# Score and state products of a small attention chained in strict alternation

## The chip, the cores and the metric

The kernel runs as one program on one core of a Trainium2 chip. The metric is the device time of one execution in microseconds (us). TensorE does the matrix products, ScalarE (ACT) the activations, VectorE (DVE) and GpSimd (POOL) the elementwise work, and SyncE (SP) issues the transfers. TensorE loads a stationary operand (PEld in the profile) and then streams a moving operand through it (PE).

## The reference

The reference is an mLSTM recurrence over 2 batches, 8 heads, 768 positions and a head dimension of 40, followed by two dense feed-forward layers over 1536 tokens (320 to 2048 and back to 320).

```python
for t in range(S):
    m_new = np.maximum(f_gate[:, :, t] + m, i_gate[:, :, t])
    f_stab = np.exp(f_gate[:, :, t] + m - m_new); i_stab = np.exp(i_gate[:, :, t] - m_new)
    C = f_stab * C + i_stab * np.einsum('bhd,bhe->bhde', vt, kt)
    n = f_stab * n + i_stab * kt
    y[:, :, t] = sigmoid(o_gate) * (C @ qt) / np.maximum(np.abs(n @ qt), 1.0)
...
h = x @ w_in;  g = h - np.tanh(h);         x1 = g @ w_out      # layer 1
h = x1 @ w_in2; g = h * np.tanh(softplus(h)); out = g @ w_out2  # layer 2
```

## The kernel before

The recurrence is computed in 12 chunks of 128 positions: 6 positions times 2 batches, in the order (position 0, batch 0), (position 0, batch 1), (position 1, batch 0) and so on. They are called chunk 0 to chunk 11 here. A chunk is one run of `attention(j)`:

- Line 309 (293 to 303 for the first two chunks) makes the decay exponents `nb` in two PSUM banks, line 312 takes their exponential into `Dm` on ACT, and line 314 masks it on POOL.
- Lines 325 to 329 make the scores `sc` = K^T Q: eight products of 64 rows by 128 columns, one for each head, into two PSUM banks. Heads 0 to 3 lie on partitions 0 to 63 and write the first bank, heads 4 to 7 lie on partitions 64 to 127 and write the second. They are called the lower and the upper half here. The data are fp32, and each product runs as two passes: 12 chunks x 8 products x 2 passes = 192 instructions.
- Line 333 multiplies each bank into `Dm` on VectorE. Line 340 makes `it` from the carried state, line 351 `pv` = `Dm` V, and lines 354 to 367 normalise, gate and store the chunk in `xo`.
- Lines 370 to 372 make the state update `st`: eight products with 40 columns of weights. Even products write PSUM partitions 0 to 39, odd ones 64 to 103. Lines 379 and 380 fold them into the state `C`.

The scores, `nb`, `it`, `pv`, `st` and the transposes `xt` (line 254) share three PSUM banks (`ps_at`) after the first two chunks. A bank is given again when the engine that reads it is done.

The dense layers run beside this. Layer 1 takes blocks of two chunks (256 tokens): `mm1` (line 506) makes `h`, `tile1` the activation on ACT, VectorE and POOL, `mm2` (lines 565 to 567) sums into `acc`. Layer 2 takes three super blocks of 512 tokens. A weight passes through VectorE and ACT once before use (`conv_w`, lines 180 to 190, `raw` into `w`).

The order of the instructions on each engine is not written out. A scheduler places them by priority and by its own estimate of times, so a new ordering edge moves much else. `tc.issue_after` (in `after`, above line 140) is such an edge: the instruction goes behind another on the same engine, without a semaphore. `w_ps` products are fill, and their results are not used.

Of the kernel before, what the change touches and what calls it, by code (L numbers as in the profile page):

```python
# [1 line left out]

# [23 lines left out]
def kernel(  # L26
# [11 lines left out]
    nc = tc.nc  # L38
    B, P, _, HG, S = qk.shape
# [7 lines left out]
    HP = P // 2  # L47
# [87 lines left out]
    def after(x):  # L135
        e = ExitStack()
        for i in x:
            e.enter_context(tc.issue_after(i.ins))
        return e

    def copy_r(eng, o, x):
        if eng == 0:
            nc.scalar.activation(out=o, in_=x, func=AF.Copy)  # L143
        elif eng == 1:
            nc.vector.tensor_copy(o, x)
        else:
            nc.gpsimd.tensor_scalar(o, in0=x, scalar1=1.0, scalar2=0.0, op0=ALU.mult, op1=ALU.add)
# [6 lines left out]
    def load_w(n=1):  # L154
        for _ in range(n):
            if pending_loads:
                layer, f = pending_loads.pop(0)
                early = layer == 0 and f < ER
                t = (xp if early else rawp).tile(
                    [P, 2 * WC], U32, tag="x" if early else "raw", name="raw", bufs=NB - 1 if early else None  # L160
                )
                with after(spq):
                    x = nc.sync.dma_start(out=t, in_=(w1, w2)[layer][f].bitcast(U32))
                if layer == 0 and f < ER + 3:
                    spq[:] = [x]
                raw[layer, f] = t
# [3 lines left out]
    def conv_w(layer, f, first=(), behind=()):  # L170
        r = raw.pop((layer, f)).rearrange("p (n t) -> p n t", t=2)
        lo32, z = r[:, :, 0], r[:, :, 1]
        zf = z.bitcast(F32)
        w = wp.tile([P, WT], F32R, tag="w", name="w")
        wf = w.bitcast(F32)

        with after(first):
            nc.vector.tensor_scalar(lo32, in0=lo32, scalar1=29, scalar2=None, op0=ALU.logical_shift_right)  # L180
        nc.vector.scalar_tensor_tensor(lo32, in0=z, scalar=0x80000000, in1=lo32, op0=ALU.bitwise_and, op1=ALU.bitwise_or)  # L181
        scaled[layer, f] = nc.scalar.activation(out=zf, in_=zf, func=AF.Copy, scale=2.0 ** -111)  # L182
        with after(behind):
            third[layer, f] = nc.vector.scalar_tensor_tensor(  # L184
                z, in0=z, scalar=3, in1=lo32, op0=ALU.logical_shift_left, op1=ALU.bitwise_or
            )
        cvd[:] = [nc.scalar.activation(out=w[:, 0:WC], in_=zf, func=AF.Copy)]  # L187
        eng = nc.gpsimd if layer == 0 and f < PRE else nc.vector
        eng.tensor_tensor(w[:, WC:WT], in0=zf[:, 0:REM0], in1=wf[:, 0:REM0], op=ALU.subtract)  # L189
        eng.tensor_tensor(w[64:P, REM0:REM1], in0=zf[64:P, REM0:REM1], in1=wf[64:P, REM0:REM1], op=ALU.subtract)  # L190
        wtile[layer, f] = w
# [43 lines left out]
    def at_ps(shape, name):  # L235
        p, tag = at_pools[0]
        if len(at_pools) > 1:
            at_pools.append(at_pools.pop(0))
        return p.tile(shape, F32, tag=tag, name=name)
# [29 lines left out]
    def attention(j):  # L269
# [3 lines left out]
        hp = lambda t, h, d=D: t[HP * (h // HG):HP * (h // HG) + d, h % HG, :]  # L273
# [14 lines left out]
        for hf in range(2):  # L288
            nb = at_ps([P, HG, L], "nb")
            flat = nb.rearrange("p g s -> p (g s)")  # L290
            if c < EC:
                bh = b * H + HG * hf
                nc.tensor.matmul(
                    flat, lhsT=na[c], rhs=sel[:, bh:bh + HG].rearrange("p (g o) -> p g o", o=1).to_broadcast([P, HG, L]),
                    start=True, stop=False,
                )
                for hh in range(HG):
                    nc.tensor.matmul(
                        nb[:, hh, :], lhsT=sel[:, bh + hh:bh + hh + 1].to_broadcast([P, P]), rhs=n0[c], start=False,
                        stop=False,  # L300
                    )

                x = nc.tensor.matmul(
                    nb, lhsT=identr, rhs=cm.rearrange("p (o s) -> p o s", o=1).to_broadcast([P, HG, L]), start=False,
                    stop=True,
                )
# [13 lines left out]
        if c + 1 < NCH:  # L320
            wv = ap_.tile([P, H, D1], F32, tag="wv", name="wv", bufs=2)
# [1 line left out]
            copy_r(2, dl, Dm[:, :, L - 1:L])  # L323
            dls[:] = [nc.gpsimd.tensor_tensor(wv, in0=v, in1=dl.to_broadcast([P, H, D1]), op=ALU.mult)]
        scs = [at_ps([P, HG, L], "sc") for _ in range(2)]
        for hh in range(HG):
            for r, sc in enumerate(scs):
                h = HG * r + hh
                x = nc.tensor.matmul(sc[:, hh, :], lhsT=hp(kT, h, HP), rhs=hp(q, h, HP), start=True, stop=True)  # L329
        yield  # L330
        for r, sc in enumerate(scs):
            d4 = Dm[:, HG * r:HG * r + HG, :]
# [4 lines left out]
        if c > 0:  # L337
            it = at_ps([P, HG, 2, D1], "it")
            for g in range(HG):
                nc.tensor.matmul(  # L340
                    it[:, g].rearrange("p h d -> p (h d)"), lhsT=q[:, g, :],
                    rhs=C[:, g].rearrange("p h d -> p (h d)"), start=True, stop=True,
# [7 lines left out]
        for h in range(H):  # L350
            x = nc.tensor.matmul(pv[:, h, :], lhsT=Dm[:, h, :], rhs=v[:, h, :], start=True, stop=True)  # L351
# [3 lines left out]
        else:  # L355
# [6 lines left out]
        x = xo[:, j, 0:DM].rearrange("p (h d) -> p h d", h=H)  # L362
        nc.vector.tensor_tensor(x, in0=hv[:, :, 0:D], in1=x, op=ALU.mult)
        gated[j] = nc.vector.scalar_tensor_tensor(
            x, in0=x, scalar=1 / WS, in1=den.to_broadcast([P, H, D]), op0=ALU.mult, op1=ALU.mult
# [2 lines left out]
        yield  # L368
        if c + 1 < NCH:
            st = at_ps([P, HG, D1], "st")  # L370
            for h in [HG * r + g for g in range(HG) for r in range(2)]:
                nc.tensor.matmul(hp(st, h), lhsT=k[:, h, :], rhs=wv[:, h, :], start=True, stop=True)
            for r in range(2):
                sl = slice(HP * r, HP * r + D)
                if c == 0:
                    copy_r(0, C[sl, :, r, :], st[sl])
                else:
                    dc = dec[sl, b, :, c:c + 1].to_broadcast([D, HG, D1])
                    nc.gpsimd.tensor_tensor(C[sl, :, r, :], in0=C[sl, :, r, :], in1=dc, op=ALU.mult)
                    nc.vector.tensor_tensor(C[sl, :, r, :], in0=C[sl, :, r, :], in1=st[sl], op=ALU.add)  # L380
# [217 lines left out]
    def program():  # L598
# [56 lines left out]
        new_xT(0, 0)  # L655

        ga, gb = (attention(j) for j in blk[0, 0])

        def go(g, n=1):
# [44 lines left out]
        def attend():  # L704
            for k in range(1, NB):
                js = blk[0, k]
                gens = [(n, attention(j)) for n, j in enumerate(js)]
                if k < NB - 1:
                    new_xT(0, k)
                loads_to(js[0] + 1)  # L710
                while gens:
                    for n, g in list(gens[:2]):
                        loads_to(js[n] + 2)
                        if next(g, 0) == 0:
                            gens.remove((n, g))
                            if k < NB - 1:
                                yield
                                transpose_x(0, k, n)
                        yield
            left.close()  # L720
            late["x"] = pool(left, "lateX", 1, reuse_waits="tile")
            late["A"] = pool(left, "lateA", 2, reuse_waits="tile")
            yield from trans(0, NB - 1)
# [163 lines left out]
```

## Time and profile before

| | us |
|---|---|
| median of 3 runs | 468.28 (468.02 to 468.96) |
| profiled execution | 467.47 |
| its span, first to last instruction | 465.6 |
| TensorE busy | 450.6 |
| VectorE busy | 320.8 |
| ACT busy | 285.6 |
| POOL busy | 115.1 |

The profile's page is one execution, and its span leaves out 1.87 us around the first and last instruction. The ends of matrix products are modelled, so TensorE counts as busy while it drains. Recurrence and layer 1 share the time up to about 284 us, layer 2 takes the rest.

### The profile page before, as it was taken

How to read it: one execution, taken by the hardware profiler on the slowest of the kernel's cores; microseconds unless marked ns; L12 is line 12 of the kernel's file. 1: busy time of each engine (PE TensorE's matmuls, PEld its weight loads, DVE VectorE, ACT ScalarE, POOL GpSimd, SP SyncE). 2: the span in 40 equal slices, each digit the busy share in tenths (PEclk: the TensorE clock that was granted, in tenths of full speed). 3: DMA queues.
4: the chain of work that ended last, by engine and by line, in shares of the span. 5: the costliest groups of instructions: out<-in, count | busy, mean ns of one | idle time of the engine just before them, and what ended most of it. 6: DMA issues, size and time to landing. Idle time of an engine off the chain costs nothing.

```text
span 465.6 us, 8007 instructions
## 1 busy us (share of the span) xinstructions
PE 450.6 (97%) x3103; PEld 408.6 (88%) x3103; DVE 320.8 (69%) x546; ACT 285.6 (61%) x518; POOL 115.1 (25%) x121
## 2 busy tenths in 40 slices
PE   9969979999999999999999999999999999999996
PEld 5646869999989999999999989998889999988995
DVE  7997999989888887666889977989932221221121
ACT  6878556596665865888889687676643333332331
POOL 3314535575354431342433332000000000000000
PEclk9997999999999999999999999999999999999999
DMA  7965454513506111000110110445301000010001
GB/s 251 356 241 163 136 164 131 179 34 109 164 4 182 34 59 63 1 1 1 63 64 0 63 63 1 132 140 175 114 1 56 2 0 1 2 56 0 1 0 56
DMA packets 22744, 38.03 MB, mean 82 GB/s; under 512 B 1364, under 2 KB 17044, under 8 KB 22708
## 3 DMA queue, kind: packets, MB, share of 16 engines
q1 hardware_dynamic: 22708, 37.54, 24.6%
q8 instruction: 24, 0.39, 0.3%
q14 instruction: 12, 0.10, 0.1%
HBM read 35.41 MB, written 1.97 MB: 80 GB/s over the span
## 4 chain that ended last, share of the span: by engine, by line
PE 61%; DVE 21%; issue 8%; ACT 4%; POOL 3%; DMA 1%; POOLq 0%; ACTq 0%; SPq 0%; DVEq 0%
PE h L506 26%; PE acc L565 8%; PE acc L566 8%; PE acc L567 8%; DVE raw L184 3%; PE sc L329 3%; DVE raw L181 2%; POOL gl L519 2%; PE pv L351 2%; DVE w L189 2%; DVE raw L180 2%; DVE w L190 2%; DVE gl L548 2%; DVE g L535 1%; DMA raw<-in_w_dram 1%
## 5 line engine op out<-in xcount | busy, mean ns | idle before, releaser
L506 PE MATMUL h<-xT,w 128*128 128x256 f32 (+1 forms) x1152 | 211.1, 324 | 5.8 <-ACT w L187 2.7
L506 PEld LDWEIGHTS h<-xT,w 128*128 128x128 f32 x1152 | 169.7, 190 | 23.4 <-ACT w L187 4.2
L565 PE MATMUL acc<-w,gh 128*128 128x320 f32 x384 | 118.6, 312 | 0.8 <-DVE xo L582 0.8
L566 PE MATMUL acc<-w,gh 128*128 128x320 f32 x384 | 118.1, 310 | 0.0
L567 PE MATMUL acc<-w,gl 128*128 128x320 f32 x384 | 108.9, 310 | 0.0
L519 POOL TENSOR_TENSOR gl<-g,gh 128x512 fp32r<-128x512 f32 x48 | 66.0, 1378 | 120.7 <-ACT gh L143 116.3
L548 DVE TENSOR_TENSOR gl<-g,gh 128x512 fp32r<-128x512 f32 x48 | 33.1, 690 | 87.1 <-ACT g L547 87.0
L546 ACT ACTIVATE gh<-h 128x512 fp32r<-128x512 f32 x48 | 28.7, 598 | 77.1 <-PE h L506 74.2
L565 PEld LDWEIGHTS acc<-w,gh 128*128 128x128 f32 x384 | 72.1, 188 | 3.5 <-ACT w L187 0.9
L566 PEld LDWEIGHTS acc<-w,gh 128*128 128x128 f32 x384 | 72.2, 188 | 2.3
L567 PEld LDWEIGHTS acc<-w,gl 128*128 128x128 f32 x384 | 69.4, 188 | 1.6 <-issue 0.4
L535 DVE COPY_PREDICATED g<-u,t 128x512 f32<-128x512 uint32 x48 | 40.4, 844 | 10.1 <-ACT u L534 9.9
L532 DVE TENSOR_TENSOR g<-u,h 128x512 f32<-128x512 f32 x48 | 32.7, 680 | 16.9 <-ACT u L531 13.4
L143 ACT ACTIVATE gh<-g 128x512 fp32r<-128x512 f32 x48 | 30.5, 635 | 19.5 <-DVE g L535 15.2
L534 ACT ACTIVATE u<-u,bias 128x512 f32<-128x512 f32 x48 | 34.9, 728 | 11.4 <-DVE g L532 11.4
L187 ACT ACTIVATE w<-raw 128x704 fp32r<-128x704 f32 x32 | 27.7, 864 | 15.5 <-DVE raw L184 15.3
L529 ACT ACTIVATE u<-h 128x512 f32<-128x512 f32 x48 | 28.5, 593 | 11.6 <-PE h L506 11.6
L182 ACT ACTIVATE raw<-raw 128x704 f32<-128x704 f32 x32 | 27.6, 864 | 11.1 <-DVE raw L181 10.0
L533 DVE TENSOR_TENSOR t<-h,t 128x512 f32<-128x512 f32 x48 | 32.7, 682 | 0.0
L184 DVE SCALAR_TENSOR_TENSOR raw<-raw 128x704 uint32<-128x704 uint32 x32 | 30.9, 966 | 2.5 <-ACT raw L182 2.3
L531 ACT ACTIVATE u<-u 128x512 f32<-128x512 f32 x48 | 30.6, 637 | 0.0
L189 DVE TENSOR_TENSOR w<-raw,w 128x576 fp32r<-128x576 f32 x30 | 27.4, 913 | 3.0 <-ACT w L187 2.5
(103 smaller groups left out, 497.7 us busy)
## 6 DMA issues: line engine op xcount, KB each, us to landing
raw<-in_w_dram SPq DMA_DIRECT2D x32, 704.0 KB
qk_t<-in_qk_dram SPq DMA_DIRECT2D x12, 512.0 KB
kv_t<-in_kv_dram SPq DMA_DIRECT2D x12, 324.0 KB
out_dram<-xo SPq DMA_DIRECT2D x12, 160.0 KB
xo<-in_og_dram SPq DMA_DIRECT2D x2, 640.0 KB
xo<-in_og_dram SPq DMA_DIRECT2D x2, 320.0 KB
sd<-nr SPq DMA_DIRECT2D x20, 4.0 KB
md<-nr SPq DMA_DIRECT2D x10, 8.0 KB
```

Of the source, the lines that this page charges most:

```text
L184: third[layer, f] = nc.vector.scalar_tensor_tensor(z, in0=z, scalar=3, in1=lo32, op0=ALU.logical_shift_left, op1=ALU.bitwise_or)
L189: eng.tensor_tensor(w[:, WC:WT], in0=zf[:, 0:REM0], in1=wf[:, 0:REM0], op=ALU.subtract)
L506: y = nc.tensor.matmul(t[:, k * nt:(k + 1) * nt], lhsT=w[:, o:o + P], rhs=x[:, kk, :], start=(n == 0), stop=(n == len(pairs) - 1),)
L519: nc.gpsimd.tensor_tensor(gl, in0=g, in1=gh.bitcast(F32), op=ALU.subtract)
L532: mark[:] = [nc.vector.tensor_tensor(g, in0=u, in1=h, op=ALU.mult)]
L533: nc.vector.tensor_tensor(t, in0=h, in1=t, op=ALU.subtract)
L534: nc.scalar.activation(out=u, in_=u, func=AF.Relu, bias=bias[:, 0:1])
L535: nc.vector.copy_predicated(out=g, mask=u.bitcast(U32), data=t)
L548: mark.append(nc.vector.tensor_tensor(gl, in0=g, in1=gh.bitcast(F32), op=ALU.subtract))
L565: nc.tensor.matmul(a, lhsT=gh[:, sl], rhs=wh, start=(f in ends_), stop=False)
L566: nc.tensor.matmul(a, lhsT=gh[:, sl], rhs=wl, start=False, stop=False)
L567: nc.tensor.matmul(a, lhsT=gl[:, sl], rhs=wh, start=False, stop=(f + 1 in ends_ or f == NF - 1))
```

## The change

The score and the state products are issued through a helper that puts each one behind the one before it on TensorE. For the scores the pairs are also turned round: the upper half goes first. The state products had the two column positions in turn in the code already. No arithmetic, tile or transfer changes.

```diff
+    @contextmanager
+    def alternate():
+        done = []
+
+        def turn(issue):
+            with after(done[-1:]):
+                done.append(issue())
+
+        yield turn
...
-        for hh in range(HG):
-            for r, sc in enumerate(scs):
-                h = HG * r + hh
-                x = nc.tensor.matmul(sc[:, hh, :], lhsT=hp(kT, h, HP), rhs=hp(q, h, HP), start=True, stop=True)
+        with alternate() as turn:
+            for hh in range(HG):
+                for r in (1, 0):
+                    h = HG * r + hh
+                    turn(lambda: nc.tensor.matmul(scs[r][:, hh, :], lhsT=hp(kT, h, HP), rhs=hp(q, h, HP), start=True, stop=True))
...
-            for h in [HG * r + g for g in range(HG) for r in range(2)]:
-                nc.tensor.matmul(hp(st, h), lhsT=k[:, h, :], rhs=wv[:, h, :], start=True, stop=True)
+            with alternate() as turn:
+                for h in [HG * r + g for g in range(HG) for r in range(2)]:
+                    turn(lambda: nc.tensor.matmul(hp(st, h), lhsT=k[:, h, :], rhs=wv[:, h, :], start=True, stop=True))
```

What the scheduler makes of it is read from the order of the instructions. The first place is TensorE at chunk 10 (161 to 165 us in the trace of before). `sc_1978` is the bank of the lower half, `sc_1979` that of the upper. Before:

```order
L309 MATMUL nb_1974<-md_96,sd1_95 128x512
L329 MATMUL sc_1978<-qk_t_1531 128x128 x4
L506 MATMUL h_1988<-xT_1515,w_351 128x256
L506 MATMUL h_1988<-xT_1515,w_359 128x256 x8
L506 MATMUL h_2055<-xT_1515,w_382 128x256 x2
L329 MATMUL sc_1979<-qk_t_1531 128x128 x4
```

and in the changed kernel:

```order
L319 MATMUL nb_1974<-md_96,sd1_95 128x512
L340 MATMUL sc_1979<-qk_t_1531 128x128
L518 MATMUL h_1988<-xT_1515,w_351 128x256
L518 MATMUL h_1988<-xT_1515,w_359 128x256 x8
L518 MATMUL h_2055<-xT_1515,w_382 128x256 x8
L340 MATMUL sc_1978<-qk_t_1531 128x128
L340 MATMUL sc_1979<-qk_t_1531 128x128
L340 MATMUL sc_1978<-qk_t_1531 128x128
L340 MATMUL sc_1979<-qk_t_1531 128x128
L340 MATMUL sc_1978<-qk_t_1531 128x128
L340 MATMUL sc_1979<-qk_t_1531 128x128
L340 MATMUL sc_1978<-qk_t_1531 128x128
```

Before, four products of one half stood together, then, behind eleven of `h`, four of the other. Now one product of the upper half stands alone, and the other seven come together, in turn. Chunks 7, 8, 9 and 11 read the same in both kernels, with other work between; so do chunks 3 and 5. Chunks 0 and 1 alternated already, and chunk 4, which had its two fours one right behind the other, alternates now in one piece of eight.

The second place is TensorE at chunk 6 (102 to 104 us). `sc_1213` is the lower half, `sc_1214` the upper. Before:

```order
L567 MATMUL acc_1042<-w_631,gl_1108 128x320
L329 MATMUL sc_1213<-qk_t_737 128x128 x3
L329 MATMUL sc_1214<-qk_t_737 128x128 x3
L329 MATMUL sc_1213<-qk_t_737 128x128
L329 MATMUL sc_1214<-qk_t_737 128x128
L565 MATMUL acc_1041<-w_641,gh_1107 128x320
```

and in the changed kernel:

```order
L340 MATMUL sc_1214<-qk_t_737 128x128
L518 MATMUL h_1284<-xT_721,w_392 128x256
L518 MATMUL h_1402<-xT_721,w_446 128x256
L340 MATMUL sc_1213<-qk_t_737 128x128
L340 MATMUL sc_1214<-qk_t_737 128x128
L340 MATMUL sc_1213<-qk_t_737 128x128
L340 MATMUL sc_1214<-qk_t_737 128x128
L340 MATMUL sc_1213<-qk_t_737 128x128
L340 MATMUL sc_1214<-qk_t_737 128x128
L340 MATMUL sc_1213<-qk_t_737 128x128
```

Here all eight products stood in one piece, partly in turn, and now one is split off in front. Chunk 2 goes the same way.

The third place is VectorE at chunk 10, where `Dm` is multiplied by the two banks and `g` and `t` belong to the activation of layer 1. Before:

```order
L532 TENSOR_TENSOR g_1946<-u_1944,h_1927 128x512
L533 TENSOR_TENSOR t_1945<-h_1927,t_1945 128x512
L333 TENSOR_TENSOR Dm_1917<-sc_1978,Dm_1917 128x512
L535 COPY_PREDICATED g_1946<-u_1944,t_1945 128x512
L333 TENSOR_TENSOR Dm_1917<-sc_1979,Dm_1917 128x512
L532 TENSOR_TENSOR g_2007<-u_2005,h_1988 128x512
L533 TENSOR_TENSOR t_2006<-h_1988,t_2006 128x512
```

and in the changed kernel:

```order
L544 TENSOR_TENSOR g_1946<-u_1944,h_1927 128x512
L545 TENSOR_TENSOR t_1945<-h_1927,t_1945 128x512
L547 COPY_PREDICATED g_1946<-u_1944,t_1945 128x512
L344 TENSOR_TENSOR Dm_1917<-sc_1979,Dm_1917 128x512
L544 TENSOR_TENSOR g_2007<-u_2005,h_1988 128x512
L545 TENSOR_TENSOR t_2006<-h_1988,t_2006 128x512
L344 TENSOR_TENSOR Dm_1917<-sc_1978,Dm_1917 128x512
```

The upper bank is read first now, and both readings stand later in VectorE's order. The state products of chunks 0 and 1 moved ahead of `pv` of their own chunk on TensorE, and elsewhere they stand as they did. On the other engines the orders move by a few positions as well, above all between chunk 2 and chunk 7.

## Rows read from the trace of the kernel before

**Rows 1.** Windows: stretch in us, its length, busy PE, PEld, DVE, ACT, POOL; clock.

```profile
40.00:60.00 20.00, 18.79 (x156) 16.30 (x156) 19.74 (x30) 11.58 (x20) 12.32 (x15) 1.00 0.46 140
60.00:80.00 20.00, 17.44 (x135) 15.14 (x135) 19.56 (x38) 13.79 (x29) 8.98 (x10) 1.00 0.47 150
80.00:100.00 20.00, 19.77 (x175) 18.70 (x175) 19.10 (x38) 13.64 (x27) 9.89 (x9) 1.00 0.44 140
120.00:180.00 60.00, 60.00 (x494) 56.73 (x493) 50.39 (x93) 38.61 (x76) 25.31 (x26) 1.00 0.26 82
220.00:260.00 40.00, 40.00 (x313) 39.99 (x312) 36.81 (x60) 33.98 (x62) 14.39 (x11) 1.00 0.16 54
```

**Rows 2.** Chain that ended last: start us, length us, work.

```profile
49.55 1.27 DVE Dm L333 x2
...
117.63 0.44 PE st L372 x16
...
161.32 1.09 PE sc L329 x8
...
182.22 1.41 PE h L506 x12
...
328.12 0.60 DVE gl L548
```

**Rows 3.** Who TensorE waited for from 180 us on: total us, times, longest.

```profile
PE acc L565 <- DVE xo L582: 0.8, 1, 0.8
PE h L506 <- ACT w L187: 0.6, 2, 0.3
```

**Rows 4.** TensorE's timeline, chunk 10: start us, length us, work, passes.

```profile
161.25 1.16 PE L329 MATMUL sc<-qk_t 64*128 64x128 f32 x8
162.34 1.55 PE L506 MATMUL h<-xT,w 128*128 128x256 f32 x11
163.82 1.16 PE L329 MATMUL sc<-qk_t 64*128 64x128 f32 x8
```

**Rows 5.** TensorE's timeline, chunk 0.

```profile
8.49 1.16 PE L329 MATMUL sc<-qk_t 64*128 64x128 f32 x16
9.58 0.33 PE L298 MATMUL nb<-n,sel 128*128 128x128 f32 x1
```

**Rows 6.** Chunk 10 cut at 161.6 and at 162.1, and its last pass alone.

```profile
161.25 0.60 PE L329 MATMUL sc<-qk_t 64*128 64x128 f32 x3
...
161.25 1.04 PE L329 MATMUL sc<-qk_t 64*128 64x128 f32 x7
...
162.14 0.27 PE L329 MATMUL sc<-qk_t 64*128 64x128 f32 x1
```

**Rows 7.** TensorE's timeline, chunk 6.

```profile
102.67 1.49 PE L329 MATMUL sc<-qk_t 64*128 64x128 f32 x16
104.08 0.41 PE L565 MATMUL acc<-w,gh 128*128 128x320 f32 x1
```

**Rows 8.** TensorE's timeline, chunks 2 and 3; in brackets idle time and releaser.

```profile
45.94 1.17 PE L329 MATMUL sc<-qk_t 64*128 64x128 f32 x16
...
50.28 1.16 PE L329 MATMUL sc<-qk_t 64*128 64x128 f32 x8 [0.83 <-DVE Dm L333]
```

**Rows 9.** TensorE's timeline, chunk 4.

```profile
68.54 2.42 PE L329 MATMUL sc<-qk_t 64*128 64x128 f32 x16 [0.46 <-ACT Dm L312]
```

**Rows 10.** The start: timelines of POOL, TensorE and VectorE.

```profile
12.32 1.28 POOL L324 TENSOR_TENSOR wv<-kv_t,dl 128x328 f32<-128x328 f32 x1
...
16.35 1.09 PE L351 MATMUL pv<-kv_t,Dm 128*128 128x41 f32 x8
...
18.45 0.15 DVE L359 TENSOR_SCALAR den<-pv 128x8 f32<-128x8 f32 x1
```

**Rows 11.** VectorE's timeline, chunk 10.

```profile
165.08 0.69 DVE L333 TENSOR_TENSOR Dm<-sc,Dm 128x512 f32<-128x512 f32 x1 [0.62 <-PE sc L329]
165.69 0.68 DVE L532 TENSOR_TENSOR g<-u,h 128x512 f32<-128x512 f32 x1
```

More of the change, by code (lines that the diff above doesn't have):

```diff
@@ L1 @@
-from contextlib import ExitStack
+from contextlib import ExitStack, contextmanager
 import concourse.bass as bass
```

## The prediction

> **What bounds the kernel now.** I read the windows first. From 40 to 100 us VectorE is the full engine: it is busy for 19.74, 19.56 and 19.10 of each 20 us, while TensorE has idle time. From about 100 us on it is the other way round: in 120 to 180 us TensorE is busy for all 60.00 us and VectorE for 50.39 [rows 1]. The chain that ended last says the same. Up to 97 us its pieces are mostly VectorE's, such as `Dm` at 49.55. Behind that nearly all are TensorE's, the scores of chunk 10 among them with 1.09 us for eight passes [rows 2]. From about 285 to 335 us the chain lies on VectorE once more, as at 328.12 [rows 2], where layer 2 starts and its weights are converted. Yet TensorE hardly stands still for it: its waits from 180 us to the end sum up to 1.4 us [rows 3]. So what is taken off TensorE behind 97 us should show in the time nearly in full, and what is taken off before should show little. Chunks 6 to 11 lie behind that point, chunks 2 to 5 before it.
>
> **What a score product costs.** The cut timeline gives the pace inside a group of one half [rows 6]. Three passes end at 161.25 + 0.60 = 161.85, seven at 161.25 + 1.04 = 162.29, so four more passes take 0.44 us: 0.11 us a pass. The third pass starts at 161.85 less a pass's own length of 0.27, that is at 161.58; the first two slots took 0.33 us, so the first alone took 0.22. The last pass starts at 162.14, and `h` follows at 162.34 [rows 4], so it holds TensorE for 0.20. A visit to the scores with n slots therefore costs 0.11n + 0.20 us: 1.08 for eight, and the rows have 162.34 - 161.25 = 1.09 [rows 4].
>
> The neighbours pay too. Eleven passes of `h` between the two visits take 163.82 - 162.34 = 1.48 us [rows 4]; at the pace of 1.41 us for twelve [rows 2] they would take 1.29. So leaving and entering again cost 0.19 us, and a visit costs about 0.39 us beyond its slots.
>
> Where the halves alternate, two passes share a slot: chunk 0 takes 9.58 - 8.49 = 1.09 us for sixteen passes [rows 5], what eight passes of one half take.
>
> On the 0.39 us: the Trainium skill, "TensorEngine Tiling (Array Packing)", Key Properties, states that a change of the tiling mode, not of the tile alone, drains TensorE. By that rule a product that is split off pays for a visit of its own, which speaks against this change. The rows agree. If no drain were paid, chunk 6 below would come out at -0.22 in place of +0.29, and the sum at -3.6 in place of -3.1.
>
> **The change, chunk by chunk.** Chunks 7 to 11 (five) had two visits of four products, 2 x 1.09 = 2.18 us. Now they have a visit of one product (two slots, 0.42) and one of seven. There the four lower products need eight slots, and the three upper ones can lie beside them: 1.09. Together 1.51, a saving of 0.67 each, 3.35 us in all; the number of visits, and so the neighbours' cost, is the same. No row shows a group of seven. At best it takes seven slots, 0.97; at worst nothing overlaps behind the lone product, 14 x 0.11 + 0.20 = 1.74. I take 1.09, since chunk 0 is the nearest row.
>
> Chunk 6 had all eight in one visit, partly in turn: 104.08 - 102.67 = 1.41 us [rows 7]. Now it is 1.51 and one visit more for the neighbours, 0.19: a loss of 0.29. Behind 97 us the sum is -3.35 + 0.29 = -3.06 us.
>
> Before 97 us: chunk 2 was already one visit of 1.17 us length like chunk 0 [rows 8, 5], and loses 1.51 + 0.19 - 1.09 = 0.61. Chunks 3 and 5 save 0.67 each. Chunk 4 had its two fours behind one another with a wait inside, 2.42 us long [rows 9] against 1.16 for a visit in turn, and saves up to 1.26. That is 2.0 us less TensorE work, but VectorE sets this stretch, so I count it at nothing. At best the change takes away all of VectorE's idle time from 40 to 100 us, 0.26 + 0.44 + 0.90 = 1.6 us [rows 1]. The other way, VectorE's new order there costs what the third rival says.
>
> The state products gain nothing: sixteen passes take 0.44 us [rows 2], 0.03 a pass, so they were in turn and overlapping already. In chunks 0 and 1 they are moved ahead of `pv`. Some 22 passes at 0.03 us put 0.6 us in front of the second `pv`. That one ends at 16.35 + 1.09 = 17.44 and VectorE reads it at 18.45 [rows 10]; this 1.0 us hides them. Without that cover the start is 0.6 us longer. `wv`, for which they wait, is ready at 13.60 [rows 10], before TensorE would come to the last of them.
>
> The two readings of `Dm` by VectorE move behind the activation that stood beside them. At chunk 10 VectorE waited for the second half of the scores anyway, 0.62 us, and took up `g` of the next tile at 165.69 [rows 11]. With the lone product and 17 passes of `h` in front, the seven start at about 161.25 + 0.42 + 17 x 0.1175 + 0.19 = 163.86 and end at 164.95, when VectorE can go on as it did. I count nothing here.
>
> **The sum.** The profiled execution took 467.47 us. Less 3.06 this is 464.4. A tenth, 0.3 us, I take as lost again in 220 to 335 us, where VectorE has only 3.2 of 40 us free [rows 1] and TensorE meets its waits [rows 3] earlier: 464.7. The median of the runs, 468.28, lies 0.8 us above the profiled execution, so the forecast for the median is 465.5, or 0.6% faster. Its own range is 463.9 to 467.1: half of the saving lost at one end, the gain before 97 us at the other.
>
> **Rivals.**
>
> 1. The stretch before 97 us gains as well. For it: TensorE idled there on VectorE and ACT, as at chunks 3 and 4 [rows 8, 9], and has 2.0 us less to do. Against: VectorE is at 97%. With 1.6 us more the time is 463.9, and with layer 2 following in full 463.6. Chance 0.16.
>
> 2. The saving is made and given back: TensorE is earlier behind 97 us, but VectorE and ACT, whose orders moved too, hand over `g`, `xo` and the converted weights no earlier. For it: VectorE at 92% in 220 to 260 us [rows 1], and the chain on it around 328 us [rows 2]. Against: only 1.4 us of waits from 180 us on [rows 3]. The 1.4 us would grow to 4.5, and the time stays at about 468.2. Chance 0.18.
>
> 3. Slower: the second bank. In the second chunk of each pair (3, 5, 7, 9, 11) one product can start once ACT has read its exponents, but the other seven stand behind the bank that VectorE frees by its `Dm` of the chunk before. Four of them ran ahead of that wait until now. TensorE issues in order, so `h` and `acc` stand behind it, and ACT and VectorE behind those. Price: chunk 3 waited 0.83 us there already [rows 8]; if the 1.09 us of the four is uncovered each time, that is 5.4 us, less 3.1 saved, and the time is 470.6. It decides from 0.6 us a pair (3.06 / 5). For it: VectorE takes `Dm` late in its new order. Against: behind 97 us TensorE did not wait once at this place. Chance 0.14.
>
> 4. It doesn't do what it says: behind the lone product the seven don't overlap. Chunks 7 to 11 stay at 0.42 + 1.74 = 2.16, chunk 6 loses 0.42 + 1.74 + 0.19 - 1.41 = 0.94, and the time is 469.1. Against it: chunk 0 [rows 5]. Chance 0.03.
>
> **How the numbers follow.** The forecast has the remaining 0.49. The range of 462.9 to 469.0 leaves out the far end of the first rival and most of the third, under 0.2 together. About 0.2%, 0.94 us, is what a measurement of this kernel can tell from no change. Faster, below 467.3, are the forecast nearly whole, the first rival and a little of the second: 0.65. Within 0.2% is the second for the most part: 0.18. Slower are the third, the fourth and the end of the second: 0.17.
>
> **What would show it.** In chunks 7 to 11 a score row of two passes should be followed 0.42 us later by other work, and one of fourteen passes 1.09 us later. If the fourteen take 1.7, the fourth rival holds. Measured from the beginning of chunk 6, layer 2 should start about 3 us earlier than before. Idle time in front of the seven, put down to `Dm`, speaks for the third rival; larger waits on `xo` or `w` behind 220 us for the second. The forecast is wrong if chunk 6, which began at 102.67 us [rows 7], begins more than 2 us later.

## The result, and the profile after

The changed kernel takes 471.47 us (median, 470.77 to 473.11), the kernel before 468.15 us beside it: ratio 1.0076, 95% interval 1.0056 to 1.0096. It is slower by 3.3 us, where 2.8 us less was forecast. The profiled execution took 470.77 us with a span of 468.2, against 467.47 and 465.6. In this section and below, medians and ratios leave out five executions that lie over 1.5% above the quickest of their kernel at a lower granted clock; each is named where it belongs.

At the scores TensorE does what was predicted. The timeline at chunk 10 (start us, length us, work, passes) has the lone product, 17 passes of `h`, and the group of seven:

```profile
163.32 0.48 PE L340 MATMUL sc<-qk_t 64*128 64x128 f32 x2
163.74 2.25 PE L518 MATMUL h<-xT,w 128*128 128x256 f32 x17
165.91 1.16 PE L340 MATMUL sc<-qk_t 64*128 64x128 f32 x14
167.00 0.42 PE L577 MATMUL acc<-w,gh 128*128 128x320 f32 x1
```

Two passes are followed 0.42 us later, fourteen 1.09 us later, where four products of one half took 1.09 before [rows 4]. Chunk 6, the one that was to lose, reads:

```profile
107.77 0.48 PE L340 MATMUL sc<-qk_t 64*128 64x128 f32 x2
108.19 0.50 PE L518 MATMUL h<-xT,w 128*128 128x256 f32 x2
108.62 1.16 PE L340 MATMUL sc<-qk_t 64*128 64x128 f32 x14
109.70 0.41 PE L577 MATMUL acc<-w,gh 128*128 128x320 f32 x1
```

But it begins at 107.77 us, not 102.67 [rows 7]. The loss lies ahead of it. The windows (stretch, its length, busy PE, PEld, DVE, ACT, POOL, then the granted clock) answer to [rows 1]:

```profile
40.00:60.00 20.00, 19.14 (x142) 16.09 (x142) 19.61 (x32) 13.12 (x23) 12.25 (x15) 1.00 0.48 152
60.00:80.00 20.00, 15.09 (x116) 12.45 (x115) 14.44 (x29) 11.10 (x23) 5.47 (x9) 0.83 0.48 157
80.00:100.00 20.00, 20.00 (x189) 19.18 (x187) 19.71 (x37) 12.83 (x24) 6.63 (x7) 1.00 0.38 111
120.00:180.00 60.00, 60.00 (x525) 56.36 (x524) 52.31 (x99) 38.81 (x76) 25.17 (x28) 1.00 0.30 89
220.00:260.00 40.00, 40.00 (x313) 39.97 (x313) 35.36 (x61) 33.75 (x62) 14.06 (x10) 1.00 0.14 46
```

In 60 to 80 us TensorE is busy for 15.09 us (17.44 before), VectorE for 14.44 (19.56 before), and the granted clock is 0.83 (1.00 before). TensorE's timeline says where it stood:

```profile
62.80 0.51 PE L384 MATMUL st<-wv,kv_t 128*40 128x41 f32 x16
66.74 0.42 PE L577 MATMUL acc<-w,gh 128*128 128x320 f32 x1 [3.43 <-ACT gh L153]
...
68.17 0.70 PE L579 MATMUL acc<-w,gl 128*128 128x320 f32 x2 [0.58 <-POOL gl L531]
...
70.00 0.47 PE L579 MATMUL acc<-w,gl 128*128 128x320 f32 x1
71.27 0.66 PE L264 MATMUL xt<-ident,xo 128*128 128x128 f32 x2 [0.80 <-DVE xo L375]
```

Behind chunk 3's state products it waits 3.43 us for the scaled operand (`gh`) of block 0's last accumulation in its first segment, which now stands ahead of chunk 3's transposes. These begin at 71.27 us, at 64.24 before.

To follow the loss further, TensorE's progress is compared. Each of its passes is given its median distance to the next in the kernel before (0.118 us for a short `h`, 0.147 for an `acc`), the scores and the fill nothing. The table tells how much later than the kernel before a kernel has done the same amount of such work. Waits, the scores' time and the clock all show in it. It is worked out from the start times in the traces; at one landmark it is good to some tenths, since neighbours change places. Kernels that keep the order of the kernel before up to 60 us (chunks 7 to 11, 6 to 11, 10, 11) stand 0.64 to 3.31 us late there all the same, by the execution that was profiled, so the differences between landmarks are what to read.

| us later than before | at 60 us | at 88 us | at 200 us | at 360 us | 88 to 200 | 200 to 360 |
|---|---|---|---|---|---|---|
| changed kernel | -0.04 | 3.42 | 0.89 | 2.80 | -2.53 | +1.91 |
| chunks 7 to 11 | 0.64 | 2.13 | -0.48 | -0.73 | -2.61 | -0.25 |
| chunks 6 to 11 | 1.57 | 0.51 | -1.62 | -1.59 | -2.13 | +0.03 |
| chunks 0, 1 | 0.14 | 7.98 | 6.86 | 7.33 | -1.12 | +0.47 |
| chunks 0 to 5 | 0.06 | 4.59 | 4.55 | 5.00 | -0.04 | +0.45 |
| chunks 4 to 11 | -0.20 | -0.31 | -2.44 | 0.95 | -2.13 | +3.39 |
| lower half first | 2.32 | -1.00 | 3.55 | 3.20 | +4.55 | -0.35 |
| filled | 0.00 | 2.80 | 0.24 | 2.44 | -2.56 | +2.20 |
| accumulation held | 0.00 | 4.82 | 3.12 | 6.14 | -1.70 | +3.02 |
| gating first | -0.03 | 2.52 | -1.11 | 0.89 | -3.63 | +2.00 |
| chunk 10 | 0.64 | 0.61 | 0.38 | 3.81 | -0.23 | +3.43 |
| chunk 11 | 3.31 | 2.23 | 1.55 | 1.74 | -0.68 | +0.19 |

The first line is the result: 3.4 us are lost at 60 to 88 us, 2.5 us gained up to 200 us, and 1.9 us lost again in layer 2. The other lines are the experiments below.

In layer 2 two waits stand out, and the kernel before has nothing of their kind near 335 us:

```profile
282.49 0.39 PE L577 MATMUL acc<-w,gh 128*128 128x320 f32 x1 [0.99 <-DVE xo L594]
...
334.86 1.17 PE L518 MATMUL h<-xT,w 128*128 128x512 f32 x4
337.55 0.41 PE L577 MATMUL acc<-w,gh 128*128 128x320 f32 x1 [1.52 <-ACT gh L558]
```

The second one comes from TensorE's own order. The accumulation stands right behind the four passes of `h` from which ACT makes its `gh`, and ACT does a weight conversion first, for which it waited itself:

```profile
336.12 0.90 ACT L192 ACTIVATE raw<-raw 128x704 f32<-128x704 f32 x1 [2.11 <-DVE raw L191]
336.88 0.62 ACT L558 ACTIVATE gh<-h 128x512 fp32r<-128x512 f32 x1
```

In the kernel before the accumulation behind such four passes reads a `gh` that was made earlier, and it does not wait:

```profile
334.74 0.60 ACT L546 ACTIVATE gh<-h 128x512 fp32r<-128x512 f32 x1
...
334.91 1.19 PE L506 MATMUL h<-xT,w 128*128 128x512 f32 x4
335.94 0.31 PE L565 MATMUL acc<-w,gh 128*128 128x320 f32 x1
```

At the first wait VectorE's `xo` comes at about the same time in both kernels (281.72 us, 281.18 before), but only nine passes of `h` stand ahead of the accumulation where the kernel before has sixteen.

### The profile page after: what moved, and what is told of

It reads as the page before. It is cut to its first block, busy times and chain, and to the rows that moved or that the text cites. A ratio compares the mean times of both kernels' runs of the same rounds, so it can differ in the third digit from the quotient of the medians.

```text
span 468.2 us, 8017 instructions
## 1 busy us (share of the span) xinstructions
PE 447.5 (96%) x3103; PEld 404.2 (86%) x3103; DVE 315.8 (67%) x546; ACT 285.9 (61%) x518; POOL 108.0 (23%) x121
## 4 chain that ended last, share of the span: by engine, by line
PE 71%; DVE 10%; DMA 9%; ACT 4%; issue 3%; POOL 1%; SPq 1%; POOLq 0%; ACTq 0%
PE h L518 31%; PE acc L577 10%; PE acc L579 9%; PE acc L578 9%; DMA raw<-in_w_dram 7%; PE pv L362 4%; PE sc L340 3%; DVE raw L191 2%; DMA xo<-in_og_dram 2%; PE it L351 2%; DVE raw L194 2%; POOL gl L531 1%; PE xt L264 1%; DVE raw L190 1%; DVE w L199 1%
## 5 line engine op out<-in xcount | busy, mean ns | idle before, releaser
L518 PE MATMUL h<-xT,w 128*128 128x256 f32 (+1 forms) x1152 | 208.1, 324 | 5.8 <-ACT w L197 2.9
L531 POOL TENSOR_TENSOR gl<-g,gh 128x512 fp32r<-128x512 f32 x48 | 64.4, 1344 | 133.5 <-ACT gh L153 127.7
L547 DVE COPY_PREDICATED g<-u,t 128x512 f32<-128x512 uint32 x48 | 38.7, 817 | 5.9 <-ACT u L546 5.8
L194 DVE SCALAR_TENSOR_TENSOR raw<-raw 128x704 uint32<-128x704 uint32 x32 | 29.8, 931 | 2.6 <-ACT raw L192 2.3
L191 DVE SCALAR_TENSOR_TENSOR raw<-raw 128x704 uint32<-128x704 uint32 x32 | 29.7, 930 | 0.4
```

The costliest lines, as they stand in the source:

```text
L194: third[layer, f] = nc.vector.scalar_tensor_tensor(z, in0=z, scalar=3, in1=lo32, op0=ALU.logical_shift_left, op1=ALU.bitwise_or)
L518: y = nc.tensor.matmul(t[:, k * nt:(k + 1) * nt], lhsT=w[:, o:o + P], rhs=x[:, kk, :], start=(n == 0), stop=(n == len(pairs) - 1),)
L531: nc.gpsimd.tensor_tensor(gl, in0=g, in1=gh.bitcast(F32), op=ALU.subtract)
L547: nc.vector.copy_predicated(out=g, mask=u.bitcast(U32), data=t)
```

## The experiments

The chains of the state products move nothing: with them alone the order on TensorE is that of the kernel before, and with the scores' chain alone it is that of the changed kernel. So the experiments are on the scores, and some of the kernels below leave the chains of the state products out. All ratios are against the kernel before, timed beside.

**1. Where the alternation may be.** Four kernels that alternate in some chunks only, or the other half first.

```diff
-        with alternate() as turn:
+        if j >= 7: # j < 2 in the second, j >= 2 in the third; else as in the kernel before
+            with alternate() as turn:
...
-                for r in (1, 0):
+                for r in (0, 1): # the fourth, all chunks
```

> Score products alternate in chunks 7 to 11 alone; chunks 0 to 6 keep the order of the kernel before, in text and in the order on TensorE. Theory (alternating is worth the predicted 0.67 us in each of these five chunks, and the loss of the changed kernel comes from the scheduler's other order at 60 to 75 us, which is not in this kernel): chunk 6's scores begin at 102.7 us as before, chunk 11's end about 3.3 us earlier than before, total 464.5 to 466.5 us. Rival 1 (alternating costs something by itself that the rows don't show): 469 us or more. Rival 2 (whatever is saved before 180 us is given back at layer 2's weight conversions): chunk 11 ends 3 us earlier, total 467.5 to 468.5 us.

Measured: 465.75 us, ratio 0.9957 (0.9936 to 0.9979). In the profiled execution chunk 6 begins at 104.60 us, not at 102.7. Chunk 11's scores do not serve as a landmark, as they stand elsewhere among `h` and `acc` (172.24 against 169.26 us at their last pass); in the table the kernel is 2.61 us faster from 88 to 200 us, and it keeps that. Its only wait of note behind 180 us:

```profile
PE h L528 <- ACT w L197: 0.8, 2, 0.5
```

The theory holds: alternation by itself does not cost, and layer 2 does not take back whatever is saved. The twelve runs go from 464.34 us (mean granted clock 0.993) to 469.07 (0.980). In the profiled one the clock fell although TensorE's order was that of the kernel before:

```profile
60.00:80.00 20.00, 17.48 (x134) 14.97 (x134) 19.20 (x38) 11.58 (x22) 8.82 (x10) 0.91 0.46 144
```

> Only the first two chunks start with the upper half and are chained (they alternate in the kernel before too, lower half first); all later chunks as before. So no slot can be saved, and the scheduler still issues block 0's last accumulation of its first segment ahead of chunk 3's transposes. Theory: the score products of chunk 4 begin 5 to 7 us later than in the kernel before, TensorE waits over 2 us for that accumulation's scaled operand, total 471 to 474 us, slower than before and no better than the changed kernel. Rival 1 (alternating itself costs): within 0.5 us of before, 467.7 to 468.7 us.

Measured: 470.54 us, just below the range, ratio 1.0063 (1.0044 to 1.0082). TensorE waits 3.9 us for the same operand, and chunk 4 begins at 76.31 us, 7.8 later than before. Up to chunk 4 no scores are saved in this kernel, so the loss at 60 to 75 us is that of the order. That none could be saved at all was not right: the scheduler put chunks 5, 7 and 9 into one visit each (chunk 7 in turn, 1.09 us, chunk 9 partly, 1.41, where two visits took 2.18) and chunk 6 into two, and the 1.12 us gained from 88 to 200 us fit that. (The profiled run, 475.07 us, is its slowest and had a clock of 0.67 at 60 to 80 us, so its 7.98 in the table is more than the usual.)

> The change in full, but not in chunks 0 and 1, which keep the order of before (lower half first). All the chains and all visits of chunks 2 to 11 are those of the changed kernel. Theory: the accumulation stays behind chunk 3's transposes, no wait of over 2 us at 60 to 70 us; chunk 6 begins at 101.5 to 103.5 us, total 464.5 to 466.5 us. Rival 1 (alternating or chaining costs): 470 to 472 us as the changed kernel. Rival 2 (given back at layer 2): 467.5 to 468.5 us.

Measured: 472.82 us, ratio 1.0105 (1.0076 to 1.0133). Against the theory, and above the first rival too. Its profiled execution had a mean clock of 0.736 and took 556.24 us, so that its rows are not used.

> The change in full with one thing turned: the chain starts with the lower half in every chunk. The order on TensorE is that of the kernel with chunks 0 and 1 unchanged, with the halves' names exchanged from chunk 2 on. Theory: 464.5 to 466.5 us, within 0.5 us of that kernel. Rival 1 (alternating or chaining costs): 470 to 472 us. A second rival for the difference (which half comes first matters by itself, since VectorE takes the lower bank first): 1 us or more between this kernel and that one.

Measured: 473.78 us, ratio 1.0121 (1.0089 to 1.0154), in its profiled run 470.94; two more runs took 479.58 and 479.77. The two kernels differ by 1.0 us, less than their runs spread (470.6 to 475.2 and 470.9 to 476.2). The theory fell in its simple form: without the moved accumulation the kernel is in front by 1.00 us at 88 us, and then loses over 5 us in the work that the kernel before does between 92 and 100 us. TensorE's waits on `gh`, `w`, `den` and `xo` come to between 1.1 and 1.5 us each from 40 to 130 us, and the clock falls in this place too, to 0.60 at 98 to 102 us and 0.55 at 102 to 106; how the loss divides between the two is not shown. That it matters which half goes first is not shown either; each of these orders has its own bad place.

**2. The wait, the clock or VectorE.** One kernel fills the wait, one moves the accumulation back, and two add further corners.

```diff
+                if j == 3:
...
+                    for _ in range(28):
+                        turn(lambda: nc.tensor.matmul(st_all[0:32, 256:512], lhsT=one[:, 0:32], rhs=one, start=True, stop=True))
```

> The changed kernel with 28 products without use (32 x 256, bf16, into the unused end of the state bank) behind chunk 3's state products, where TensorE waits 3.43 us in the changed kernel. The order on TensorE is otherwise that of the changed kernel; VectorE has one weight conversion a place earlier and ACT two copies. It parts the loss at 60 to 75 us into the wait and the fall of the clock behind it. Theory: the clock falls because TensorE stands still; filled, it stays at 1.00, the bias products and the accumulations of 68 to 74 us run at full speed, chunk 6 begins 1.5 to 3 us earlier than in the changed kernel (at 104.8 to 106.3 us), total 468 to 470 us: still slower than before, by the wait. Rival 1 (VectorE, busy 3.9 of 4 us there, sets the time, so that the clock is hidden): clock 1.00, but total 470.5 to 471.5 us. Rival 2 (the fall has nothing to do with the lull): clock under 0.9 at 60 to 80 us as before, total 471 us or more.

Measured: 472.53 us, ratio 1.0073 (1.0047 to 1.0099); its two quickest runs 470.40 (the profiled one) and 470.68 at a clock of 0.993. By the median it lies above all three ranges; the other four runs had a clock of 0.985 to 0.989. The timeline and the window of the filled kernel:

```profile
63.29 3.28 PE L389 MATMUL st<-const-bfloat16-1.0 128*32 128x256 bf16 x28
...
71.50 0.41 PE L264 MATMUL xt<-ident,xo 128*128 128x128 f32 x2 [1.46 <-DVE xo L375]
```

```profile
60.00:80.00 20.00, 17.08 (x155) 13.79 (x156) 15.45 (x29) 11.10 (x23) 6.07 (x9) 1.00 0.50 156
```

In this execution the clock stays at 1.00, and chunk 3's transposes still begin at 71.50 us, chunk 6 at 107.12. The trace speaks for the first rival: the clock's fall is nearly hidden here, since TensorE waits for VectorE's `xo`. Nor is the clock the cause of the whole loss: five runs of the kernel before beside this one, at 0.992 to 0.994, take 467.79 to 468.45 us, and the two filled ones at 0.993 are still some 2.5 us above them.

```diff
+        held = ExitStack()
+        if i == 3:
+            held.enter_context(after([turned[0, 3]]))  # chunk 3's last transpose
...
+        held.close()
```

> The changed kernel with one edge more: block 0's last accumulation of the first segment goes behind chunk 3's transposes again. The scheduler moves later work too (chunk 4's scores in one piece of eight and one alone, chunks 5 to 11 in other places). Theory: the transposes no longer stand behind the wait for the scaled operand; chunk 4's scores begin at 69 to 72.5 us (75.47 in the changed kernel, 68.54 before), total 465.5 to 469 us if no other wait of over 2 us comes in its place between 75 and 100 us. Rival 1 (alternating itself costs): 470.5 us or more with no wait of over 1 us on the rows. Rival 2 (any other order in this stretch costs some 3 us or more, since VectorE is full there): chunk 4 in time, but chunk 6 later than 105 us, 469 to 473 us.

Measured: 474.14 us, ratio 1.0115 (1.0089 to 1.0141); a sixth run took 730.82 us at a mean clock of 0.554. With the accumulation out of the way the transposes themselves wait:

```profile
71.14 0.66 PE L265 MATMUL xt<-ident,xo 128*128 128x128 f32 x2 [7.79 <-DVE xo L377]
```

They begin at 71.14 us, as in the changed kernel, and chunk 4 at 77.18. All three expectations are wrong, and so was the theory: the moved accumulation only covered part of a wait for VectorE.

```diff
+        if j >= 4: # j < 6 in the second
+            with alternate() as turn:
```

> The change from chunk 4 on; chunks 0 to 3 keep the order of before, and with them everything on TensorE up to 68 us. Theory in its simple form (only the moved accumulation costs): chunk 4's scores begin at 68.5 to 69.3 us, chunk 6's at 101.5 to 103.5 us, total 464.5 to 466 us. Rival 2 (any other order between 68 and 100 us costs): chunk 6 begins at 105 us or later, total 468.5 to 473 us.

Measured: 468.43 us, ratio 0.9998 (0.9980 to 1.0016). Chunk 4 begins at 68.33 us, chunk 6 at 99.87, even earlier than the range. At 200 us the kernel leads by 2.44 us, and then loses 3.39 us in layer 2. Neither expectation had that.

> The change in chunks 0 to 5 alone; from chunk 6 on the scores keep the two-by-four form of before. It is the fourth corner beside before, the changed kernel and the kernel that alternates in chunks 7 to 11 alone. Theory (the early order costs what chunk 6's beginning shows, the late alternation gives 0.67 us in each of five chunks, and the two add up): chunk 4 and the wait of over 3 us as in the changed kernel, chunk 6 at 107 to 109 us, total 2.3 to 3.3 us above the changed kernel, 473 to 475 us. Rival (the late saving is lost in the changed kernel, so that only the early order counts): within 0.7 us of the changed kernel, 470.8 to 472.2 us.

Measured: 472.86 us, ratio 1.0090 (1.0061 to 1.0119); a sixth run took 562.97 us at a mean clock of 0.733. It is 1.4 us above the changed kernel by the medians, between the two expectations. Chunk 6 begins at 108.89 us, as the theory has it. From 88 to 200 us it gains 0.04 us, where the changed kernel gains 2.53; but its layer 2 costs 0.45 us in place of 1.91. So the late saving is there, and the order of layer 2 is another term.

**3. VectorE's order at 60 to 71 us.** Behind chunk 3's `hv` the kernel before has the gating first (timeline of VectorE):

```profile
61.01 0.49 DVE L354 TENSOR_TENSOR hv<-hv,pv 128x328 f32<-128x328 f32 x1
...
63.51 0.48 DVE L364 SCALAR_TENSOR_TENSOR xo<-xo,den 128x320 f32<-128x320 f32 x1
63.93 0.69 DVE L532 TENSOR_TENSOR g<-u,h 128x512 f32<-128x512 f32 x1
```

and the changed kernel an activation and the weight conversions:

```profile
60.82 0.50 DVE L365 TENSOR_TENSOR hv<-hv,pv 128x328 f32<-128x328 f32 x1 [0.26 <-PE pv L362]
61.40 0.69 DVE L544 TENSOR_TENSOR g<-u,h 128x512 f32<-128x512 f32 x1
62.01 0.68 DVE L545 TENSOR_TENSOR t<-h,t 128x512 f32<-128x512 f32 x1
62.61 0.95 DVE L190 TENSOR_SCALAR raw<-raw 128x704 uint32<-128x704 uint32 x2
...
65.25 0.72 DVE L547 COPY_PREDICATED g<-u,t 128x512 f32<-128x512 uint32 x1
65.86 0.88 DVE L191 SCALAR_TENSOR_TENSOR raw<-raw 128x704 uint32<-128x704 uint32 x1
...
67.35 1.51 DVE L191 SCALAR_TENSOR_TENSOR raw<-raw 128x704 uint32<-128x704 uint32 x1
68.79 0.15 DVE L371 TENSOR_TENSOR den<-hv,den 128x8 f32<-128x8 f32 x1
68.87 0.88 DVE L194 SCALAR_TENSOR_TENSOR raw<-raw 128x704 uint32<-128x704 uint32 x1
...
69.83 0.90 DVE L194 SCALAR_TENSOR_TENSOR raw<-raw 128x704 uint32<-128x704 uint32 x1
70.64 0.48 DVE L375 SCALAR_TENSOR_TENSOR xo<-xo,den 128x320 f32<-128x320 f32 x1
```

`hv` is ready at the same time in both, 61 us. The gated `xo`, on which chunk 3's transposes wait, comes 7.1 us later. One edge puts it back; the scheduler then also sets the conversions behind the gating and the transposes ahead of the accumulation, so that this piece of order is tried as a whole:

```diff
-        mark[:] = [nc.vector.tensor_tensor(g, in0=u, in1=h, op=ALU.mult)]
+        with after([gated[3]] if i == 3 else []):
+            mark[:] = [nc.vector.tensor_tensor(g, in0=u, in1=h, op=ALU.mult)]
```

> The changed kernel with one edge on VectorE: the first product of the activation of tile 3 (`g`, at 61.40 us in the changed kernel) goes behind chunk 3's last gating step (`xo`). The scheduler then also puts the weight conversions behind it, as in the kernel before, and chunk 3's transposes in front of block 0's last accumulation. Theory (second form: chunk 3's gating is 7.1 us late because VectorE does an activation and three conversion steps first, and TensorE only waits for it): `xo` of chunk 3 at 62.5 to 64.5 us instead of 70.64, no wait of over 2 us on TensorE at 60 to 75 us, chunk 4's scores begin at 67 to 70 us, chunk 6's at 100 to 104 us; by 200 us TensorE is 1.5 to 3 us ahead of the kernel before; total 464.5 to 466.5 us if layer 2 gives nothing back, 467.5 to 469.5 us if its order there costs the 2 to 3 us that it cost with the changed and the held kernel. Rival (the late gating is not the cause): chunk 4 at 74 us or later, total 470.5 us or more.

Measured: 468.60 us, ratio 0.9999 (0.9980 to 1.0017), 2.9 us below the changed kernel. VectorE and TensorE:

```profile
64.15 0.49 DVE L375 SCALAR_TENSOR_TENSOR xo<-xo,den 128x320 f32<-128x320 f32 x1
64.67 0.69 DVE L545 TENSOR_TENSOR g<-u,h 128x512 f32<-128x512 f32 x1
```

```profile
64.79 0.41 PE L264 MATMUL xt<-ident,xo 128*128 128x128 f32 x2 [1.47 <-DVE xo L375]
```

Chunk 4 begins at 69.21 us (75.47 in the changed kernel, 68.54 before). The second form of the theory holds, and the time is the one that was given for a layer 2 that gives back: 2.00 us in the table. At 200 us the lead is 1.11 us, not 1.5 to 3, and chunk 6 begins at 104.52: this execution's clock fell too, to 0.74 of full speed in 60 to 80 us. At 88 us the table has the kernel still 2.52 us late, only 0.90 less than the changed kernel. TensorE does not wait at 67 to 78 us; its passes are slower, as these fourteen show, here and in the kernel before:

```profile
73.30 3.21 PE L518 MATMUL h<-xT,w 128*128 128x256 f32 x14
```

```profile
70.89 1.90 PE L506 MATMUL h<-xT,w 128*128 128x256 f32 x14
```

So it is the times, not this trace, that show what the edge is worth. At a like clock, 0.981 to 0.986, five of its runs take 468.46 to 469.03 us and the changed kernel's four 470.77 to 473.11.

```diff
-        if j >= 7:
+        if j >= 6:
             with alternate() as turn:
```

> Chunks 6 to 11 alternate; the order of everything else is that of the kernel in which chunks 7 to 11 do. Chunk 6 goes from one visit of 16 passes with three of one half on end (1.41 us) to one lone product and a visit of 14. By the visits' prices 0.25 to 0.3 us slower than the kernel with chunks 7 to 11: 464.8 to 466.2 us, still 2 us below before. If a lone visit costs more than its 0.42 us in this place, 466.5 us or more.

Measured: 466.06 us, ratio 0.9941 (0.9919 to 0.9964), 0.3 us above the kernel of chunks 7 to 11, though both spread more than that. As expected.

**4. Layer 2.** Two kernels that differ from the kernel before in one chunk each. With chunk 10 the order of layer 2 up to 340 us becomes that of the changed kernel, with chunk 11 it stays that of the kernel before.

```diff
-        if j >= 7:
+        if j == 10: # j == 11 in the second
             with alternate() as turn:
```

> Chunk 10 alone alternates. Up to chunk 10 the order on TensorE is that of the kernel before, so nothing can be lost there; the order of layer 2's first half (280 to 340 us) becomes that of the changed kernel. It asks whether the 1.9 us that the changed kernel loses between 270 and 340 us belong to that order. Theory (they do, whatever was saved earlier): TensorE is 0.4 to 0.8 us ahead of before at 200 to 260 us and 1 to 2.5 us behind it at 345 us, with waits of over 1 us at the accumulation near 280 and near 335 us; total 469 to 470.5 us, slower than before with less than a microsecond of other work moved. Rival (layer 2 only gives back what was saved, since VectorE sets the time there): 467.8 to 468.5 us, as before, and no such waits beyond before's.

Measured: 470.78 us, ratio 1.0050 (1.0033 to 1.0068), all six runs within 470.6 to 471.7. From 88 to 200 us the kernel gains 0.23 us, less than the 0.4 to 0.8 of the theory, since chunk 11 fell into three visits; from 200 to 360 us it loses 3.4 us. TensorE's waits from 180 to 345 us:

```profile
PE acc L587 <- ACT gh L568: 1.5, 1, 1.5
PE acc L587 <- DVE xo L604: 1.0, 1, 1.0
```

They are the two waits of the changed kernel. Next to nothing was saved that could be given back, so the rival falls: this loss belongs to the order. The kernel of chunks 4 to 11 has the same order of layer 2 on TensorE, the same two waits, 1.5 and 1.0 us, and loses 3.39 us there.

> Chunk 11 alone alternates. The order on TensorE is that of the kernel before up to chunk 11, and in layer 2 too. Theory (one chunk of this kind is worth 0.67 us, and this order of layer 2 gives little back): ahead by 0.5 to 0.8 us at 200 us and by 0.3 to 0.8 us at 345 us, total 467.1 to 467.7 us. Rival (layer 2 gives back what was saved): ahead at 200 us, level at 345 us, total 467.8 to 468.3 us.

Measured: 468.11 us, ratio 1.0006 (0.9986 to 1.0027). By the median this is the rival's figure, but the runs go from 466.78 us at a clock of 0.993 to 470.72 at 0.981. The five at 0.993 or 0.994 have a median of 466.89 us, where twelve of the kernel before at 0.992 to 0.994 have 467.82: that speaks for the theory. In the profiled one the clock was 0.83 at 40 to 60 us, where this kernel has the order of the kernel before. Behind that it gains 0.68 us up to 200 us and gives back 0.19: what the theory says of the trace.

## Why the prediction was wrong

The price of the scores was right. For each visit the stretch from the pass ahead of the last neighbour to the pass behind the next, less the neighbours' usual distances, was added up. Chunks 7 to 11 went from 12.78 to 9.39 us, -3.39 where -3.35 was predicted; chunks 6 to 11 from 14.40 to 11.38, -3.02 where -3.06 was. A lone product costs 0.61 us with its neighbours, so the 0.39 us beyond its two slots of 0.11 stand; a group of seven costs 1.28. This agrees with the drain at a change of the tiling mode that the Trainium skill, "TensorEngine Tiling (Array Packing)", Key Properties, states. No idle time stands in front of a group of seven behind 97 us, so the third rival was not it, and the fourteen passes take 1.09 us, so neither was the fourth. (The prediction's aside on a kernel without drains, -0.22 us for chunk 6 and -3.6 in all, counts seven slots for the group of seven where its sum counts eight; with eight it is -0.11 and -3.5. Nothing rests on it.) The earlier start of the state products in chunks 0 and 1 cost nothing.

The step that failed is the one before 97 us: "VectorE sets this stretch, so I count it at nothing". The reading was right, that VectorE is full there and TensorE waits for it. The conclusion was not. Where VectorE is full, what counts is the order of its work, and the prediction looked for that only in the two readings of `Dm`. It took the lower bound there from the third rival, a wait for the second bank, and from nothing that VectorE might do first. The gating of chunk 3 went behind an activation and the conversions of two weights, 7.1 us, and TensorE lost 3.4 us at 60 to 88 us; with the gating back in its place the time is 2.9 us less. That VectorE's new order should be read as a whole was in reach, since it stood in the order of the changed kernel; the prediction compared TensorE's rows and let VectorE's go. It did name the sign by which it would fall: chunk 6 over 2 us later. It was 5.1.

The second miss is the term of 0.3 us "lost again in 220 to 335 us": it measured 1.9. The second rival had this place, with TensorE waiting for `g`, `xo` and the weights, but with operands that come no earlier than before and so with the time of before as its end. The kernel with chunk 10 alone shows that it isn't a ceiling: the order there costs 3.4 us with nothing saved, and with the order of the kernel before the 2.6 us that chunks 7 to 11 had saved by 200 us were all kept.

So the sum was 3.4 - 2.5 + 1.9 = 2.8 us in place of -2.8; 2.5 and not 3.0 because from 88 to 200 us the distances at the scores fall by 3.18 us, while the waits over 0.14 us grow from 0.55 to 1.10 (one of 0.95 at 101 us is new) and the rest by 0.10. The larger of the two waits in layer 2 is made by an accumulation that stands right behind its own `h`, as shown above. What stays open is what in the chain makes the scheduler choose these orders: a change in chunk 10 alone is enough for the one, one in chunks 0 and 1 for the other.

The better kernel is the one that alternates in chunks 6 or 7 to 11 alone: 466.06 and 465.75 us, 0.4 to 0.6% faster than before. There the order of layer 2 stayed that of the kernel before. Nothing in the edit asks for that, and chunk 10 alone turned it the other way, so this part is luck.

## What to carry to other kernels

Under a scheduler an ordering edge has two prices: what it does at its place, which the rows give well, and what it makes of all the other orders, which can be larger and of either sign. Before counting a stretch at nothing because another engine is full there, read that engine's new order and ask which of its results the waiting engine now gets last. And apply such an edge only where the engine it serves is the bound: here in five or six of twelve chunks. Even there each placement has to be measured, since chunk 10 alone, in that stretch, made the kernel 2.9 us slower.

## What was not expected of the hardware

In the changed kernel TensorE was busy for 1.31 and 2.68 of two stretches of 4 us, and its clock fell to half in the second and the ones behind it:

```profile
62.00:66.00 4.00, 1.31 (x22) 1.00 (x21) 3.90 (x11) 1.10 (x2) 0.00 (x0) 1.00 0.83 240
66.00:70.00 4.00, 2.68 (x12) 2.42 (x12) 3.94 (x8) 2.58 (x4) 1.29 (x1) 0.80 0.01 4
70.00:74.00 4.00, 3.09 (x9) 1.71 (x9) 3.17 (x7) 3.93 (x11) 0.88 (x2) 0.50 0.21 41
74.00:78.00 4.00, 4.00 (x35) 3.75 (x35) 1.78 (x3) 1.02 (x2) 3.31 (x7) 0.84 0.84 330
```

The granted clock of 0.50 is 1.2 GHz of 2.4. With products without use in the wait it stayed at 1.00 in the profiled execution; four of that kernel's six runs had a mean clock of 0.985 to 0.989 all the same, so that the filling prevents the fall is not shown. What the fall costs depends on what TensorE waits for: some 0.6 us here by the table (2.80 in place of 3.42 us late at 88 us when filled), while over the runs of one kernel, the one with chunks 7 to 11, a mean clock of 0.980 to 0.982 goes with 2.7 to 3.9 us more than the 465.14 us that its runs at 0.993 have as their median. The same kernel shows the fall in some executions and not in others, so that two kernels that differ by 1 us can't be told apart by a few runs unless the clock is read beside the time.
